# A hand-written scheduler counts TensorE's latency, gets more exponential slots and a new order in the second layer

## The chip, the cores and the metric

The kernel runs on one core of a Trainium2 chip, in one launch. The metric is the device time of a whole execution in microseconds. An engine is one of TensorE (PE; its weight loads are shown apart as PEld), VectorE (DVE), ScalarE (ACT), GpSimd (POOL) and SyncE (SP, which here only issues DMAs).

## The reference

Two layers, with the same weights in both. Each adds an attention block and then a token-mixing MLP to x, which is 2048 tokens by 512 features in bf16:

```python
x = x + _A_ref(_layernorm(x), A_wqkv, A_wo)            # attention
x = x + _B_ref(_layernorm(x), B_w1, B_b1, B_w2, B_b2)  # MLP over the tokens
x = x + _A_ref(_layernorm(x), A_wqkv, A_wo)
x = x + _B_ref(_layernorm(x), B_w1, B_b1, B_w2, B_b2)
```

The attention has 32 heads of width 16 and a sliding window: a query sees itself and the 255 tokens before it. The MLP normalises once more, multiplies along the token axis with w1 (2048 to 1792), adds b1, applies the tanh form of gelu, multiplies with w2 (1792 to 2048), adds b2, and the result is added to x.

## The kernel before

**Tiling.** x lies in 16 tiles of 128 tokens (`x_sb`), its normalised form in `xh_sb`, the transposed normalised form in `xhT` (two buffers of 512 tokens). Attention goes in quarters Q of 512 queries. In a quarter there are four groups t of eight heads and for each nine steps m, so 36 steps a quarter, 144 a layer, 288 in all. A step is three things in turn:

- `emit_scores` (line 581): TensorE computes scores in 64x64 cells of its array, into two of four PSUM banks; two steps alternate between the halves.
- `emit_exp` (line 592): one exponential on ScalarE over both banks, into one of NSLOT slots of `p_sb` (line 268; step n takes slot n modulo NSLOT), and then multiplications with the edge mask (line 609), on GpSimd or VectorE.
- `emit_pv` (line 630): TensorE multiplies the slot with V, adding up over the nine steps in banks 4 and 5. After the ninth, VectorE copies both banks out (line 319), and small DMAs bring the denominators together (`den_c`).

**Jobs beside the steps.** `job_k`, `job_q` (matmuls at line 454) and `job_v` (line 500) make projections, which VectorE or ScalarE masks and writes out (lines 464, 469); `job_normalise` and `job_outproj` (548) finish the quarter before; `job_transpose` fills `xhT`, at the very start through TensorE and afterwards by a DMA transpose that SP issues (line 435). They all share PSUM banks 6 and 7 in turn. In the MLP, `u_product` (752) makes the first product, some of it ahead of time in the last attention quarter, and `job_y` (789) the second: 14 matmuls for one tile of 128 output tokens, in two operations of 10 and 4. Four y products of the first layer are done in the dense stage, four at the seam of the layers, and eight inside the second layer's attention (tiles 8 to 11 and 12 to 15).

**What sets the order.** Every operation goes into `Plan` with a cost in ns for each engine that could do it, its reads and writes, and a priority. `Plan.arrange` then walks through all of them before the program is built: it keeps a clock for each engine, takes the engine that can go on first, and there the operation of lowest priority among those that are ready within 60 ns. TensorE has three modes (full, columns for V, cells for scores, PV and normalising), and an operation in another mode than the last counts as 1.0 later in priority and 100 ns longer. The result is a fixed order for each engine; on the chip semaphores hold the dependences, and an operation of TensorE that depends on an earlier one of TensorE waits for no semaphore. The line of the walk that the change touches is 151: `lat`, the time from an operation's end until a dependent may start, is 80 ns, and 200 for TensorE's operations, but before the change 0 from TensorE to TensorE.

**Priorities.** A step is 5/9 of a unit, a quarter 20 units, and the second layer begins at unit BASE = 400. Scores come EARLY = 1.0 unit ahead of a step's position, PV 1.6 behind it. `span_jobs` spreads a quarter's jobs evenly over 19 units in a written order ("k1" is the K projection of group 1, "K0" that of the next quarter's group 0, "v" the V projections of the next quarter, "o" the output projections of the quarter before), and `beside` says at which job the transposes are issued. The warm-up (line 394) is 13 blocks of ten small matmuls in bank 4, at -7.2, while the first inputs come in. `constants` has GpSimd write the ones beside V (`put_ones`), build `spread` (memset and 16 selects, lines 831 and 838) and load the two bias vectors (line 844).

Of the kernel before, what the change touches and what calls it, by code (L numbers as in the profile page):

```python
# [10 lines left out]
P = 128  # L11
EARLY = 1.0
PV_LAG = 1.6
FIRSTV = -0.7
WARM = 13
NPART = 4
PARTQ = (0, 1)
# [1 line left out]
MASKED = 1215  # L19
XPOS = 0.7  # L20
XSTEP = 1.2
NORM0 = 6.5
XLAT = 1500
SPAN0 = 0.3
SPAN = 19.0

# [13 lines left out]
class Plan:  # L40
# [53 lines left out]
    def arrange(self):  # L94
# [12 lines left out]
        todo = len(self.ops)  # L107
        while todo:
            best = None
            for e in self.ENGS:  # L110
                if not pool[e]:
                    continue
                t = max(free[e], min(o.ready for o in pool[e]))
                if best is not None and t >= best[0]:
                    continue
                pick = None
                for o in pool[e]:
                    if o.ready > t + 60:
                        continue
                    if any(max(free[x], o.ready) + w[0] + self.SPARE.get(x, 0) <  # L120
                           max(t, o.ready) + o.on[e][0] + self.SPARE.get(e, 0) for x, w in o.on.items() if x != e):
                        continue
                    key = (o.prio + (self.STAY if e == "tensor" and o.mode != mode else 0), o.num)
                    if pick is None or key < least:
                        pick, least = o, key
                if pick is not None:
                    best = (max(t, pick.ready), e, pick)
            if best is None:
                cand = min(((max(free[e], o.ready) + o.on[e][0] + self.SPARE.get(e, 0), o.num, e, o) for e in self.ENGS for o in pool[e]),
                           key=lambda v: v[:2])  # L130
                e, pick = cand[2], cand[3]
                best = (max(free[e], pick.ready), e, pick)
            t, e, o = best
            o.eng, o.start = e, t
            free[e] = t + o.on[e][0]
            if e == "tensor":
                if o.mode != mode:
                    free[e] += self.SWITCH
                mode = o.mode
            if o.dma:  # L140
                bus = max(bus, free[e]) + o.dma / 200
                o.end = bus + 1600
            else:
                o.end = free[e]
            line[e].append(o)
            for x in o.on:
                pool[x].remove(o)
            todo -= 1
            for s in o.succ:
                s.left -= 1  # L150
                s.ready = max(s.ready, o.end + (0 if e == "tensor" and e in s.on else o.lat))
                if not s.left:
                    for x in s.on:
                        pool[x].append(s)
# [80 lines left out]
def bass_interleave_layers__sliding_block__mixer_token_mlp__prompt_kernel(  # L235
# [16 lines left out]
    NQ = S // 512  # L252
    NFT = F // P
    EPS = 1e-5
    SMSCALE = 1.0 / math.sqrt(DH)
    NSLOT = 5

    es = ExitStack()
    with es:
# [171 lines left out]
        def job_transpose(Q, i, prio):  # L431

            t, buf = 4 * Q + i, Q % 2
            if prio > 0:
                plan.op({SP: (600, lambda e: e.dma_start_transpose(xhT[:, buf, :, i * P:(i + 1) * P], xh_sb[:, t, :]))},
                        reads=[R("xh", t)], writes=[R("xhT", buf, i)], prio=prio, dma=1 << 17, lat=XLAT)
                return
            b = misc_bank()
            pv = ps[:, b, :].bitcast(dt.bfloat16)
# [19 lines left out]
        def masked(b, prio, dst, src, mask, key, writes):  # L459
# [7 lines left out]
            def each(e):  # L467
                for h in range(2):
                    last = e.activation(dst[:, :, h], src, ACTF.Copy, scale=mask[:, h:h + 1])
                return last  # L470
            plan.op({ACT: (1380, each)} if key == "even" and prio < 0 else {DVE: (MASKED, both), ACT: (1380, each)}, reads=[R(key)], shares=[BK(b)], writes=writes, prio=prio)

        def job_k(Q, t, prio):

# [34 lines left out]
        def first_jobs(p0, dp):  # L509

            jobs = [lambda p, i=i: job_transpose(0, i, p) for i in range(4)] + [lambda p: job_k(0, 0, p), lambda p: job_q(0, 0, p)]
            return ([(p0 + dp * n, job) for n, job in enumerate(jobs)] +
                    [(p0 + 9 + FIRSTV + 0.3 * i, lambda p, i=i: job_v(0, i, p)) for i in range(4)])

        def span_jobs(Q, p0):


            order = ["k1", "q1", "v0", "v1", "k2", "q2", "v2", "o0", "k3", "q3", "o1", "v3", "K0", "Q0", "o2", "o3"]
            beside = {"q1": (0, 1), "q2": (2,), "k3": (3,)} if Q + 1 < NQ else {}
            if Q == 0:  # L520
                order = [j for j in order if j[0] != "o"]
            if Q == NQ - 1:
# [161 lines left out]
        def attention(L, base):  # L684
            todo, n = [], 0
            for Q in range(NQ):
                for t in range(4):
                    for m in range(NB):
# [4 lines left out]
                        todo.append((p0, step))  # L693
                        todo.append((p0 + PV_LAG, lambda p, a=(Q, t, m, n % NSLOT): emit_pv(*a, p)))
                        n += 1
                todo += span_jobs(Q, base + 20 * Q)
            end = base + 20 * NQ
            todo.append((end + 3, lambda p: job_inverse(NQ - 1, p)))
            for t in range(2):
# [120 lines left out]
                ln_stats(t, p)  # L820
            ln_apply(g, False, p)
        for g in range(NQ):
            todo.append((-20 if g == 0 else 18 * g - 19, lambda p, g=g: first_norm(g, p)))

        def constants(p):
            for n in range(2, 5):
                for i in range(2):
                    put_ones(n, i, p + 5 * n, [R("xh", 3)], (POOL,))


            setup(lambda e: e.memset(spread[:], 0.0), 530, reads=[R("xh", 3)], writes=[R("spread")], prio=p)
# [19 lines left out]
        for L in range(2):  # L851
# [23 lines left out]
                        todo.append((base + 126, lambda p, n=n, i=i: put_ones(n, i, p, engines=(POOL,), writes=[R("v", n, i, h) for h in range(2)])))  # L875
            for st in range(NT):
                p, b = base + 131 + st, st % 6
                if L == 0 and 4 <= st < 8:
                    p = BASE - 9 + 2.2 * (st - 4)
                elif L == 0 and st >= 8:  # L880
                    p = BASE + (8 + 3 * (st - 8) if st < 12 else 26 + 3 * (st - 12))
                    b = None
                todo.append((p, lambda p, st=st, b=b, L=L: job_y(st, misc_bank() if b is None else b, L, p)))
        todo.sort(key=lambda v: v[0])
        for p, job in todo:
# [32 lines left out]
```

## Time and profile before

| | |
|---|---|
| median of 3 runs | 533.8 us (533.21 to 535.61) |
| the profiled execution | 534.36 us, of which the span of instructions is 532.6 |
| granted TensorE clock, mean | 0.997 |
| first layer, attention (first to last exponential) | 17.7 to 177.8 us |
| then dense MLP and the seam of the layers | to 252.8 us |
| second layer, attention | 252.8 to 434.3 us |
| then dense MLP to the end | 532.6 us |

The mean exponential of full width (128 x 1024) takes 1.03 us on ScalarE. By quarter, from the first exponential of one to the first of the next, the time is 39.3, 41.6, 38.8 and 40.4 us in the first layer and 46.7, 54.4, 40.0 and 40.4 us in the second; the exponentials of a quarter are busy for 29.3 us in a first quarter, where they are shorter, and 36.8 to 37.1 us in the others. Busy times of TensorE overlap, since its matmuls are pipelined, so they say more as a comparison of stages than as a share.

### The profile page before, as it was taken

The page shows a single profiled execution, that of the slowest core. Times are in us where ns is not written, and L with a number is a line of the kernel's source. Part 1 is how long each engine was busy: PE and PEld are TensorE (multiplying, and loading weights), DVE is VectorE, ACT ScalarE, POOL GpSimd, SP SyncE. Part 2 cuts the span into 40 slices and gives each one's busy share as a digit, 9 for nine tenths or more (in the row PEclk, how much of TensorE's full clock was granted, in tenths as well). Part 3 has the DMA queues.
Part 4 walks back from the last instruction along what each step waited for, and adds up shares of the span by engine and source line. Part 5 has one row for each costly group of instructions (what it writes and reads, how often), then busy time and mean ns, then how long its engine had stood idle before and what let it go on. Part 6 is the DMA issues. An engine that isn't in the chain of part 4 may idle for free.

```text
span 532.6 us, 21297 instructions
## 1 busy us (share of the span) xinstructions
PE 484.0 (91%) x9540; PEld 273.7 (51%) x9618; DVE 318.7 (60%) x539; ACT 296.1 (56%) x335; POOL 234.4 (44%) x468
## 2 busy tenths in 40 slices
PE   7779889989889899999889888988998989999997
PEld 7455555655555444445545555555645544444443
DVE  5778869868767361157756767596876655221222
ACT  5757887988888304300746766479888860230000
POOL 5976864756665301101735644276565540200000
PEclk9999999999999999999999999999999999999999
DMA  6192515210135430533203410032221635053631
GB/s 198 45 121 66 103 44 97 72 45 25 45 96 158 124 108 0 138 103 78 43 3 94 105 31 25 3 53 73 83 65 57 192 113 149 1 140 97 180 113 44
DMA packets 84443, 44.38 MB, mean 83 GB/s; under 512 B 20864, under 2 KB 83328, under 8 KB 84352
## 3 DMA queue, kind: packets, MB, share of 16 engines
q1 hardware_dynamic: 80480, 43.00, 30.7%
q0 software_dynamic: 3872, 0.02, 1.9%
q8 instruction: 75, 1.23, 1.0%
q14 instruction: 16, 0.13, 0.1%
HBM read 32.51 MB, written 2.10 MB: 65 GB/s over the span
## 4 chain that ended last, share of the span: by engine, by line
PE 72%; DVE 12%; issue 7%; POOL 5%; ACT 3%; SPq 1%; DMA 0%; POOLq 0%; ACTq 0%; DVEq 0%
PE ps L789 18%; PE ps L752 18%; PE ps L581 9%; PE ps L454 8%; PE ps L630 8%; PE ps L548 5%; PE ps L500 4%; ACT p_sb L592 3%; DVE q_sb L464 2%; POOL p_sb L609 2%; DVE k_sb L464 1%; DVE xh_sb L417 1%; DVE oU L319 1%; POOL rstd L410 1%; PE ps L674 1%
## 5 line engine op out<-in xcount | busy, mean ns | idle before, releaser
L592 ACT ACTIVATE p_sb<-ps 128x1024 bf16<-128x1024 f32 (+8 forms) x288 | 261.3, 972 | 104.1 <-PE ps L581 96.3
L609 POOL TENSOR_TENSOR p_sb<-p_sb,edge 128x128 bf16<-128x128 bf16 (+2 forms) x361 | 171.8, 480 | 137.5 <-ACT p_sb L592 126.2
L581 PE MATMUL ps<-q_sb,k_sb 64*64 64x288 bf16 (+8 forms) x2816 | 106.9, 251 | 10.7 <-ACT p_sb L592 5.4
L630 PE MATMUL ps<-p_sb,v_all 64*64 64x288 bf16 (+8 forms) x2816 | 94.9, 248 | 11.1 <-POOL p_sb L609 6.0
L581 PEld LDWEIGHTS ps<-q_sb,k_sb 64*64 64x64 bf16 x2816 | 54.1, 106 | 60.5 <-ACT p_sb L592 29.7
L630 PEld LDWEIGHTS ps<-p_sb,v_all 64*64 64x64 bf16 x2816 | 58.4, 107 | 27.5 <-POOL p_sb L609 15.6
L793 DVE SCALAR_TENSOR_TENSOR x_sb<-ps,b2col,x_sb 128x512 bf16<-128x512 f32 x32 | 24.0, 750 | 76.0 <-PE ps L789 75.9
L454 PE MATMUL ps<-xhT,wqkv 128*128 128x512 bf16 x216 | 58.2, 384 | 9.8 <-issue 7.4
L789 PE MATMUL ps<-uT,w1buf 128*128 128x512 bf16 x274 | 61.8, 379 | 1.3 <-DVE rc L658 0.8
L464 DVE TENSOR_TENSOR k_sb<-ps,half 128x1024 bf16<-128x1024 f32 x32 | 39.0, 1218 | 16.1 <-PE ps L454 16.0
L752 PE MATMUL ps<-xh_sb,w1buf 128*128 128x512 bf16 x182 | 43.3, 379 | 2.0 <-issue 0.6
L400 DVE BATCH_NORM_STATS2 stats<-x_sb 128x6 f32<-128x512 bf16 x64 | 43.5, 688 | 1.1
L789 PEld LDWEIGHTS ps<-uT,w1buf 128*128 128x128 bf16 x280 | 26.8, 98 | 33.4 <-issue 1.8
L464 DVE TENSOR_TENSOR v_all<-ps,even 128x1024 bf16<-128x1024 f32 x29 | 35.1, 1217 | 11.5 <-PE ps L500 10.9
L464 DVE TENSOR_TENSOR q_sb<-ps,even 128x1024 bf16<-128x1024 f32 x31 | 37.7, 1217 | 4.5 <-PE ps L454 4.3
L410 POOL TENSOR_TENSOR rstd<-vare,mhalf 128x4 f32<-128x4 f32 x16 | 16.2, 1014 | 50.5 <-DVE nmean L412 50.4
L500 PE MATMUL ps<-wqkv,xhT 128*32 128x128 bf16 x2048 | 34.7, 220 | 3.7 <-issue 2.6
L789 PE MATMUL ps<-uT,oU 128*128 128x512 bf16 x165 | 36.8, 379 | 0.2
L454 PEld LDWEIGHTS ps<-xhT,wqkv 128*128 128x128 bf16 x256 | 20.5, 98 | 30.3 <-issue 7.8
L500 PEld LDWEIGHTS ps<-wqkv,xhT 128*32 128x32 bf16 x2048 | 29.1, 97 | 9.9 <-issue 7.2
L779 ACT ACTIVATE uT<-ps,b1col 128x512 bf16<-128x512 f32 x20 | 13.3, 689 | 36.8 <-PE ps L752 36.8
L548 PE MATMUL ps<-wo_sb,oT 128*128 128x512 bf16 x117 | 29.9, 380 | 2.9 <-DVE oT L681 1.7
(67 smaller groups left out, 396.2 us busy)
## 6 DMA issues: line engine op xcount, KB each, us to landing
w1buf<-in_B_w_dram SPq DMA_DIRECT2D x10, 896.0 KB
oU<-in_B_w_dram SPq DMA_DIRECT2D x6, 896.0 KB
w1buf<-in_B_w_dram SPq DMA_DIRECT2D x10, 512.0 KB
oU<-o SPq DMA_DIRECT2D x16, 256.0 KB
k_sb<-in_B_w_dram SPq DMA_DIRECT2D x16, 256.0 KB
xhT<-in_B_w_dram SPq DMA_DIRECT2D x8, 256.0 KB
q_sb<-in_B_w_dram SPq DMA_DIRECT2D x8, 256.0 KB
out_dram<-x_sb SPq DMA_DIRECT2D x16, 128.0 KB
```

The costliest lines, as they stand in the source:

```text
L400: dve(lambda e: e.bn_stats(stats[:, t, :], x_sb[:, t, :]), 690, prio, reads=[R("x", t)], writes=[R("stats", t)])
L454: last = e.matmul(ps[:, b, :], lhsT=wqkv[:, c, c0:c0 + P], rhs=xhT[:, buf, c, :], start=(c == 0), stop=(c == 3))
L464: return e.tensor_tensor(dst, src.unsqueeze(2).to_broadcast([P, n, 2, w]), mask[:].unsqueeze(1).unsqueeze(3).to_broadcast([P, n, 2, w]), o ...
L500: last = e.matmul(acc[32 * a:32 * a + 32, k], lhsT=xhT[:, buf, c, t0:t0 + 32], rhs=wv[:, c, :, a, :], start=(k == 0 and c == 0), stop=(k = ...
L548: last = e.matmul(ps[:, b, :], lhsT=oT[:, buf, t, i * P:(i + 1) * P], rhs=wo_sb[:, t, :], start=(t == 0), stop=(t == 3))
L581: last = e.matmul(ps[64 * c:64 * c + 64, 2 * half + r, 32 * i0:32 * i1], lhsT=k_sb[rows, ring, t, kb % 16, :], rhs=q_sb[rows, t, c, 32 * i ...
L592: latest[0] = plan.op({ACT: (170 + int(2 * (512 - c0) * 0.84), lambda e: e.activation(p_sb[:, slot, :, c0:512], ps[:, 2 * half:2 * half + ...
L609: return e.tensor_tensor(v, v, g, op=ALU.mult)
L630: last = e.matmul(ps[64 * r:64 * r + 64, B_O + (c ^ r), 32 * i0:32 * i1], lhsT=v_all[rows, col:col + 64], rhs=p_sb[rows, slot, r, 32 * i0: ...
L752: r = e.matmul(ps[:, b, :], lhsT=blk[:, n, (ft % 2) * P:(ft % 2 + 1) * P], rhs=xh_sb[:, 4 * g + n, :], start=(first and g == quarters[0] a ...
L789: r = e.matmul(ps[:, b, :], lhsT=blk[:, fc, (st % 2) * P:(st % 2 + 1) * P], rhs=uT[:, fc, :], start=(fc == 0), stop=(fc == NFT - 1))
L793: dve(lambda e: e.scalar_tensor_tensor(x_sb[:, st, :], ps[:, b, :], b2col[:, st:st + 1], x_sb[:, st, :], op0=ALU.add, op1=ALU.add), 750, prio,
```

## The change

Seven things are changed:

- In the walk, a dependence from TensorE to TensorE now counts the 200 ns too.
- NSLOT is 7 instead of 5.
- A DMA transpose takes 1230 ns of SP in the walk and has the usual latency of 80, instead of 600 and 1500.
- `spread` and the bias loads have a priority 10 units later.
- In the second layer `span_jobs` has an order of its own, in which all K and Q projections come first and V jobs alternate with output projections; the four transposes are issued together at "q3". The last quarter keeps its order.
- y products of the first layer that lie in the second layer's attention have new positions: tiles 8 to 11 at 10, 13, 16 and 19 units (before: 8, 11, 14, 17) and tiles 12 to 15 at 31, 34, 37 and 40 (before: 26, 29, 32, 35). Tiles 4 to 7 stay.
- FIRSTV, VACT and NORM1 become parameters, with values that give what was written out before.

```diff
@@ -11,7 +11,13 @@
 P = 128
 EARLY = 1.0
 PV_LAG = 1.6
-FIRSTV = -0.7
+FIRSTV = (-0.7, -0.4, -0.1, 0.2)
+VACT = 0
+NORM1 = -1
+SPREADP = 10
+ORDER1 = "k1 q1 k2 q2 k3 q3 v0 o0 v1 o1 o2 v2 o3 v3 K0 Q0"
+BES1 = {"q3": (0, 1, 2, 3)}
+YP = ((-9, 2.2), (10, 3), (31, 3))
 WARM = 13
 NPART = 4
 PARTQ = (0, 1)
@@ -20,7 +26,6 @@
 XPOS = 0.7
 XSTEP = 1.2
 NORM0 = 6.5
-XLAT = 1500
 SPAN0 = 0.3
 SPAN = 19.0
 
@@ -148,7 +153,7 @@
             todo -= 1
             for s in o.succ:
                 s.left -= 1
-                s.ready = max(s.ready, o.end + (0 if e == "tensor" and e in s.on else o.lat))
+                s.ready = max(s.ready, o.end + o.lat)
                 if not s.left:
                     for x in s.on:
                         pool[x].append(s)
@@ -253,7 +258,7 @@
     NFT = F // P
     EPS = 1e-5
     SMSCALE = 1.0 / math.sqrt(DH)
-    NSLOT = 5
+    NSLOT = 7
 
     es = ExitStack()
     with es:
@@ -432,8 +437,8 @@
 
             t, buf = 4 * Q + i, Q % 2
             if prio > 0:
-                plan.op({SP: (600, lambda e: e.dma_start_transpose(xhT[:, buf, :, i * P:(i + 1) * P], xh_sb[:, t, :]))},
-                        reads=[R("xh", t)], writes=[R("xhT", buf, i)], prio=prio, dma=1 << 17, lat=XLAT)
+                plan.op({SP: (1230, lambda e: e.dma_start_transpose(xhT[:, buf, :, i * P:(i + 1) * P], xh_sb[:, t, :]))},
+                        reads=[R("xh", t)], writes=[R("xhT", buf, i)], prio=prio, dma=1 << 17)
                 return
             b = misc_bank()
             pv = ps[:, b, :].bitcast(dt.bfloat16)
@@ -468,7 +473,7 @@
                 for h in range(2):
                     last = e.activation(dst[:, :, h], src, ACTF.Copy, scale=mask[:, h:h + 1])
                 return last
-            plan.op({ACT: (1380, each)} if key == "even" and prio < 0 else {DVE: (MASKED, both), ACT: (1380, each)}, reads=[R(key)], shares=[BK(b)], writes=writes, prio=prio)
+            plan.op({ACT: (1380, each)} if key == "even" and prio < VACT else {DVE: (MASKED, both), ACT: (1380, each)}, reads=[R(key)], shares=[BK(b)], writes=writes, prio=prio)
 
         def job_k(Q, t, prio):
 
@@ -510,13 +515,16 @@
 
             jobs = [lambda p, i=i: job_transpose(0, i, p) for i in range(4)] + [lambda p: job_k(0, 0, p), lambda p: job_q(0, 0, p)]
             return ([(p0 + dp * n, job) for n, job in enumerate(jobs)] +
-                    [(p0 + 9 + FIRSTV + 0.3 * i, lambda p, i=i: job_v(0, i, p)) for i in range(4)])
-
-        def span_jobs(Q, p0):
+                    [(p0 + 9 + FIRSTV[i], lambda p, i=i: job_v(0, i, p)) for i in range(4)])
+
+        def span_jobs(Q, p0, L):
 
 
             order = ["k1", "q1", "v0", "v1", "k2", "q2", "v2", "o0", "k3", "q3", "o1", "v3", "K0", "Q0", "o2", "o3"]
             beside = {"q1": (0, 1), "q2": (2,), "k3": (3,)} if Q + 1 < NQ else {}
+            if L == 1 and ORDER1:
+                order = ORDER1.split()
+                beside = {} if Q + 1 == NQ else BES1
             if Q == 0:
                 order = [j for j in order if j[0] != "o"]
             if Q == NQ - 1:
@@ -693,7 +701,7 @@
                         todo.append((p0, step))
                         todo.append((p0 + PV_LAG, lambda p, a=(Q, t, m, n % NSLOT): emit_pv(*a, p)))
                         n += 1
-                todo += span_jobs(Q, base + 20 * Q)
+                todo += span_jobs(Q, base + 20 * Q, L)
             end = base + 20 * NQ
             todo.append((end + 3, lambda p: job_inverse(NQ - 1, p)))
             for t in range(2):
@@ -820,12 +828,13 @@
                 ln_stats(t, p)
             ln_apply(g, False, p)
         for g in range(NQ):
-            todo.append((-20 if g == 0 else 18 * g - 19, lambda p, g=g: first_norm(g, p)))
+            todo.append((-20 if g == 0 else 18 * g - 18 + NORM1, lambda p, g=g: first_norm(g, p)))
 
         def constants(p):
             for n in range(2, 5):
                 for i in range(2):
                     put_ones(n, i, p + 5 * n, [R("xh", 3)], (POOL,))
+            p += SPREADP
 
 
             setup(lambda e: e.memset(spread[:], 0.0), 530, reads=[R("xh", 3)], writes=[R("spread")], prio=p)
@@ -875,11 +884,10 @@
                         todo.append((base + 126, lambda p, n=n, i=i: put_ones(n, i, p, engines=(POOL,), writes=[R("v", n, i, h) for h in range(2)])))
             for st in range(NT):
                 p, b = base + 131 + st, st % 6
-                if L == 0 and 4 <= st < 8:
-                    p = BASE - 9 + 2.2 * (st - 4)
-                elif L == 0 and st >= 8:
-                    p = BASE + (8 + 3 * (st - 8) if st < 12 else 26 + 3 * (st - 12))
-                    b = None
+                if L == 0 and st >= 4:
+                    p0, dp = YP[st // 4 - 1]
+                    p = BASE + p0 + dp * (st % 4)
+                    b = None if p >= BASE else b
                 todo.append((p, lambda p, st=st, b=b, L=L: job_y(st, misc_bank() if b is None else b, L, p)))
         todo.sort(key=lambda v: v[0])
         for p, job in todo:
```

## The prediction

> **What bounds the kernel now.** I read the page first, then the busy times in ten stretches cut where the exponentials of one quarter of an attention layer begin (36 steps each), then ScalarE's and TensorE's timelines inside the bad stretches.
>
> ```profile
> span 532.6 us, 21297 instructions
> PE 484.0 (91%) x9540; PEld 273.7 (51%) x9618; DVE 318.7 (60%) x539; ACT 296.1 (56%) x335; POOL 234.4 (44%) x468
> ```
>
> The 91% is a mean over stages with different limits, so it decides nothing. The stretches do (columns: length, then busy PE, PEld, DVE, ACT, POOL, clock):
>
> ```profile
> 17.70:57.00 39.30, 32.25 (x914) 19.34 (x912) 30.64 (x55) 29.25 (x42) 29.16 (x74) 0.96 0.64 82
> 98.60:137.40 38.80, 35.08 (x1084) 22.71 (x1084) 29.48 (x45) 34.66 (x37) 24.62 (x45) 1.00 0.15 47
> 177.80:252.80 75.00, 74.53 (x544) 34.86 (x549) 31.51 (x57) 11.87 (x16) 8.61 (x12) 1.00 0.33 90
> 252.80:299.50 46.70, 41.45 (x972) 24.24 (x974) 31.80 (x48) 27.18 (x36) 25.36 (x68) 1.00 0.24 59
> 299.50:353.90 54.40, 48.88 (x1197) 29.17 (x1207) 37.77 (x60) 34.73 (x38) 27.00 (x50) 1.00 0.13 29
> 434.30:532.60 98.30, 94.65 (x502) 42.91 (x509) 26.67 (x44) 11.04 (x15) 3.75 (x6) 1.00 0.36 103
> ```
>
> The dense stages (third and last row) are TensorE without a gap, 49 matmuls in 10.74 us on the chain, or 219 ns each: an order can win nothing there. A plain quarter (second row) has 34.7 us of ScalarE in 38.8: the exponentials, 36 of 1.03 us, are its floor. The two quarters of the second layer that carry four y products each take 46.7 and 54.4 us although ScalarE is busy for 27.2 and 34.7 and TensorE idles 5 us in each: neither engine is the bound, they take turns. The timeline shows how:
>
> ```profile
> 270.71 3.20 PE L789 MATMUL ps<-uT,w1buf 128*128 128x512 bf16 x14
> 273.96 0.81 PE L454 MATMUL ps<-xhT,wqkv 128*128 128x512 bf16 x3
> 275.07 1.14 ACT L592 ACTIVATE p_sb<-ps 128x576 bf16<-128x576 f32 x2 [3.41 <-PE ps L581]
> 284.40 2.33 PE L789 MATMUL ps<-uT,w1buf 128*128 128x512 bf16 x10
> 286.67 0.43 PE L581 MATMUL ps<-q_sb,k_sb 64*64 64x288 bf16 x8
> 287.03 1.14 ACT L592 ACTIVATE p_sb<-ps 128x576 bf16<-128x576 f32 x2 [1.68 <-PE ps L581]
> 287.71 0.81 PE L789 MATMUL ps<-uT,w1buf 128*128 128x512 bf16 x3 [0.16 <-issue]
> 288.91 2.69 ACT L592 ACTIVATE p_sb<-ps 128x1024 bf16<-128x1024 f32 x3 [0.74 <-PE ps L581]
> ```
>
> A whole y product (14 matmuls in one piece) holds TensorE for 3.2 us and ScalarE starves for 3.41. One of the eight happens to be cut into its 10 and its 4, with scores between: 1.68 + 0.74 = 2.42. The other six whole ones cost 1.87, 2.55, 2.86, 4.41, 3.53 and 4.18: the mean of the seven is 3.26.
>
> The first quarter has a loss of its own:
>
> ```profile
> 39.24 1.04 PE L454 MATMUL ps<-xhT,wqkv 128*128 128x512 bf16 x2 [2.58 <-issue]
> 40.90 1.89 ACT L592 ACTIVATE p_sb<-ps 128x1024 bf16<-128x1024 f32 x2 [4.02 <-PE ps L581]
> 40.00:44.00 4.00, 4.00 (x81) 2.13 (x84) 3.17 (x4) 2.25 (x3) 1.47 (x4) 0.68 0.02 4
> ```
>
> TensorE stands 2.58 us inside a product, waiting for nothing shown, and then runs at a granted 0.68. Just before, from 32.5 to 36.2 us, the two bias loads moved 3872 packets of 4 bytes; TensorE's instruction-fetch packets of 16 KB, normally 4 to 7 us apart here, start at 29.7 and only then at 36.8.
>
> **The change, part by part.** The sum is made against the profiled execution, 534.36 us (span 532.6 and 1.8 around it), 0.6 above the median of 533.8. Edits that leave every value as it was (FIRSTV, VACT, NORM1) cost nothing.
>
> *TensorE's 200 ns in the walk.* The walk now holds a TensorE operation back for 200 ns after the one it depends on. At the start, the 13 warm-up blocks form such a chain. By the code's costs (three of 1070, ten of 540, now 200 between) the first transpose is ready when ten are placed, not thirteen; one more falls among the transposes, one before the first K and one before the first Q. In the trace the blocks run to 10.34 and the transposes begin at 10.40, though their first input was normalised by about 9.0. A block is about 0.56 us, so K can start up to 1.5 us sooner and Q, with one block ahead of it, 0.9. Q gates the first scores: **-0.9** (0 to -1.5).
>
> In the y products the gap lies between the 10 and the 4. If scores take it, a whole y goes from 3.26 to 2.42 us of starving: 7 x 0.84 = 5.9. But the walk adds 1.0 to the priority of anything that changes TensorE's mode, so another K or Q product, if one is ready, takes the gap instead; four of the eight y products are followed directly by a K, Q or output projection now. Half: **-3.0** (0 to -5.9). The four pairs of u products that run in one piece (one followed by 1.81 us of ScalarE idle, another by 1.39) give **-0.5**.
>
> The same gap lies between any two PV operations. The order of weight loads in the trace has 106 of 288 PVs directly behind another. What fills the gap is scores if ScalarE has freed a bank, else a projection, ahead of the scores it used to follow. One product more before the scores costs 0.5 us where it shows (0.51 to 0.58 in four places). How often is not in the trace: between none and thirty, 0 to +15. I take three, **+1.5**, because the products are the same in number and two banks limit how far they run ahead.
>
> Each change of mode also costs. Four projection matmuls followed by another full product take 0.86 us, followed by scores 0.97: 0.11. Seven cuts are 14 changes at most, 1.5 us, mostly inside TensorE's 5 us of idle per quarter: **+0.5**. The Trainium skill (TensorEngine Tiling (Array Packing), Key Properties) says that changing the tiling mode drains the engine, which speaks against every cut; the trace agrees, at 0.11 us. Without that price the sum is 0.5 lower.
>
> *Seven slots.* ScalarE waits for a PV, that is for a slot, six times: 1.02 in the first quarter, then 0.92, 0.79, 0.82, 0.75 and 1.52, together 4.8. With 7 slots the next exponential needs a PV two steps older. But PVs wait there for VectorE's copies out of their two banks, which stay: half, **-2.4** (0 to -4.8).
>
> *Spread and bias loads 10 units later.* GpSimd's selects no longer go before the edge masks: the first PV waits 0.86 us for one, and the exponential behind it 1.02. VectorE is busy 4.00 of 4.00 us from 24 to 28, so it is late next: **-0.5** (0 to -1.0). The bias loads move with them, past masks on GpSimd's queue (their two issues hold it 1.3 and 1.2 us). The stall of 2.6 us comes back if a fetch falls due in their 3.7 us; at 4 to 7 us between fetches that is more likely than not, but with a shorter delay on average: **-1.5** (-4.0 to +2.6). The Trainium skill (Runtime: NRT & Kernel Launch, Instruction fetch mechanics) has fetches in blocks of 16 KB, mostly hidden; the trace has the 16 KB packets, and a stall beside a late one.
>
> *Second layer's order, y later.* The amount of work is the same. V pairs that run in one piece (1.9 us at 264.2 and at 305.5, the latter followed by 1.38 of ScalarE idle) come apart. The fourth y of each group slides towards the next quarter, where TensorE idles 4 of 40 us. Against it, three or four y products gather in a half quarter with four V jobs. **-1.0** (-3 to +3). V must precede the next quarter's first PV at unit 21.6; V3 at 15.7 leaves six units, some 14 us.
>
> *Transposes.* SP's row is 1.24 us for each and their packets end 2.0 us after issue begins; the walk's new 1230 + 655 + 1600 + 80 is still longer, the old 4355 more so. No V will wait: **0**. The four now go in one burst past the den_c loads on SP, 5 us, hidden by the 6 units above.
>
> Sum: -0.9 - 3.0 - 0.5 + 1.5 + 0.5 - 2.4 - 0.5 - 1.5 - 1.0 = -7.8, so 526.6 for a profiled execution and **526.0** for the median.
>
> **Rivals.**
> *The gaps go to projections (slower).* If thirty of the 106 PV gaps take a product ahead of scores, 30 x 0.52 = +15.6 in place of the +1.5 gives 526.0 + 14.1 = 540. It decides from about 18 such places (7.8 + 1.5 over 0.52). For it: the walk's delay is not the chip's (two PVs back to back take 0.46 us, two single ones 0.22 each). Against: only two banks feed products.
> *Nothing that can be told.* Projections take the y gaps too, the slots' waits reappear as VectorE's copies, the fetch stall recurs: left are the start and half of the rest, -2, 532. Under 0.5% (2.7 us) no measurement of this kernel tells a change; the changed constants would then have done what they say for nothing.
> *The stall is no fetch.* Then moving the bias loads returns 0: 526.0 + 1.5 = 527.5. This is also what the Trainium skill's word "hidden" would make of it. For it: shorter unexplained stops elsewhere (1.60 us at 266.4). Against: the packets' times.
>
> **How the numbers follow.** Forecast 0.45, no fetch 0.12, nothing to tell 0.17, projections 0.26. So faster 0.57, same 0.17, slower 0.26. The range: down to the forecast with the y cut, slots and bias terms nearly whole (-3, -2.4, -2.5 more: 518), up to 541, the slower rival and 1; about 0.2 is outside.
>
> **What would show it.** Fewer than 13 warm-up blocks before the first transpose, and the first exponential near 16.8 instead of 17.74. y products in 10 and 4 with scores between, and the second layer's first two quarters below 46.7 and 54.4 us. No ScalarE wait ended by a PV. TensorE without a 2.6 us stop near 36 to 45 us. Dense stages unchanged. Wrong if plain quarters grow beyond 41.6 us with projections between PVs, or those two stay at 101 us together.

## The result, and the profile after

The changed kernel takes 525.97 us (median of 4, 525.07 to 528.41) where the kernel before took 534.59 (median of 4): a ratio of 0.9853 [0.9832, 0.9875], so about 1.5% faster, or 7.8 us of 533.8. (The two medians alone would give 0.984; the text goes by the ratio.) The forecast was 526.0. The profiled execution took 525.07 us, span 523.3, 9.3 us less than the 532.6 before. The mean granted clock was 0.997 before and 0.999 after, so the clock explains next to nothing; only in the first quarter do the rows differ, 0.96 before and 1.00 after.

The page after, span and engines:

```profile
span 523.3 us, 21380 instructions
PE 492.1 (94%) x9618; PEld 275.1 (53%) x9618; DVE 317.6 (61%) x533; ACT 297.7 (57%) x337; POOL 236.3 (45%) x473
```

The same work as before in a shorter span: only the shares rise. Where the 9.3 us went is seen in the stretches cut as before (columns: length, then busy PE, PEld, DVE, ACT, POOL, clock). These are the first and third quarter of the first layer, the dense stage with the seam, the second layer's first three quarters, and the dense end:

```profile
18.30:54.00 35.70, 32.30 (x1001) 20.37 (x990) 32.30 (x50) 28.10 (x40) 29.86 (x78) 1.00 0.66 102
95.40:135.10 39.70, 36.76 (x1037) 22.41 (x1032) 30.76 (x46) 34.58 (x36) 24.79 (x45) 1.00 0.15 45
173.30:249.60 76.30, 75.36 (x551) 34.86 (x549) 31.39 (x60) 11.87 (x16) 9.18 (x14) 1.00 0.33 89
249.60:293.10 43.50, 41.57 (x976) 23.86 (x972) 29.75 (x42) 27.39 (x36) 25.41 (x69) 1.00 0.20 46
293.10:342.90 49.80, 46.43 (x1177) 27.55 (x1172) 37.10 (x60) 34.81 (x36) 27.35 (x49) 1.00 0.16 42
342.90:386.00 43.10, 40.77 (x1166) 24.81 (x1158) 34.75 (x52) 35.81 (x39) 27.42 (x50) 1.00 0.33 66
424.90:523.30 98.40, 95.35 (x512) 42.91 (x510) 26.67 (x44) 11.02 (x15) 3.75 (x6) 1.00 0.36 103
```

The first quarter fell from 39.2 to 35.7, the second layer's first two from 46.7 and 54.4 to 43.5 and 49.8, and its third rose from 40.0 to 43.1. The dense stages did not gain: the end is 98.3 and 98.4, the seam 75.1 and 76.3. To two decimals, from exponential to exponential, in us:

| | first exp. | first layer, quarters 1 to 4 | seam | second layer, quarters 1 to 4 | end |
|---|---|---|---|---|---|
| before | 17.74 | 39.23, 41.62, 38.78, 40.38 | 75.10 | 46.69, 54.33, 40.03, 40.37 | 98.34 |
| after | 18.28 | 35.69, 41.41, 39.76, 38.12 | 76.34 | 43.55, 49.79, 43.02, 38.90 | 98.48 |
| change | +0.54 | -3.54, -0.21, +0.98, -2.26 | +1.24 | -3.14, -4.54, +2.99, -1.47 | +0.14 |

The changes add up to -9.3: -5.0 in the first layer's attention, -6.2 in the second's, +1.9 elsewhere. They are those of one execution each: the first quarter takes 37.1 to 39.2 us in four kernels in which no edit touches the first layer (the kernel before, `b_order_y`, `b_ypos`, `b_order1`).

ScalarE's waits have the slots' part (columns: engine, its operation, who it waited for; us in total, times, longest). Before, then after:

```profile
ACT p_sb L592 <- PE ps L581: 96.3, 83, 26.2
ACT p_sb L592 <- PE ps L630: 5.8, 6, 1.5
```

```profile
ACT p_sb L600 <- PE ps L589: 90.6, 86, 27.2
ACT p_sb L600 <- PE ps L638: 0.6, 1, 0.6
```

Each first row is the wait for scores (26.2 and 27.2 us of it is one wait through the dense stage), each second the wait for a PV, that is for a slot: 5.8 us have become 0.6, and without the long wait the one for scores fell from 70.1 to 63.4. So both kinds of starving shrank. That this fits the forecast's sum does not show that its terms were right; the experiments took them one by one. Every ratio below is against the kernel before, run on the same chip; the first four experiments shared one chip, the next four another, and the rest ran on two more, so a difference between ratios of different groups is an estimate. Medians count every run, while the ratios leave out four that were slow: 533.34 us of `a_nolat_y`, 534.78 of `b_order1`, and 580.93 and 588.31 of `b_bias90` (granted clock 0.85 and 0.82).

### The profile page after: what moved, and what is told of

The parts are those of the page before. It is cut to its first block, busy times and chain, and to the rows that moved or that the text cites. A ratio compares the mean times of both kernels' runs of the same rounds, so it can differ in the third digit from the quotient of the medians.

```text
span 523.3 us, 21380 instructions
## 1 busy us (share of the span) xinstructions
PE 492.1 (94%) x9618; PEld 275.1 (53%) x9618; DVE 317.6 (61%) x533; ACT 297.7 (57%) x337; POOL 236.3 (45%) x473
## 4 chain that ended last, share of the span: by engine, by line
PE 79%; DVE 8%; POOL 3%; issue 3%; ACT 3%; DMA 2%; SPq 1%; POOLq 0%; DVEq 0%; ACTq 0%
PE ps L760 19%; PE ps L797 19%; PE ps L589 10%; PE ps L459 9%; PE ps L638 9%; PE ps L556 6%; PE ps L505 5%; ACT p_sb L600 2%; PE ps L399 2%; POOL p_sb L617 2%; DMA oU<-o 1%; PE ps L682 1%; DVE oT L689 1%; DVE o L324 1%; DVE q_sb L469 1%
## 5 line engine op out<-in xcount | busy, mean ns | idle before, releaser
L617 POOL TENSOR_TENSOR p_sb<-p_sb,edge 128x256 bf16<-128x256 bf16 (+2 forms) x366 | 173.1, 478 | 127.5 <-ACT p_sb L600 116.2
L589 PE MATMUL ps<-q_sb,k_sb 64*64 64x288 bf16 (+8 forms) x2816 | 108.5, 250 | 7.2 <-ACT p_sb L600 6.0
L638 PE MATMUL ps<-p_sb,v_all 64*64 64x288 bf16 (+8 forms) x2816 | 104.9, 247 | 10.7 <-issue 3.4
L638 PEld LDWEIGHTS ps<-p_sb,v_all 64*64 64x64 bf16 x2816 | 60.1, 107 | 30.9 <-POOL p_sb L617 13.2
L459 PE MATMUL ps<-xhT,wqkv 128*128 128x512 bf16 x256 | 65.9, 381 | 1.9 <-DVE v_all L469 0.8
L797 PE MATMUL ps<-uT,w1buf 128*128 128x512 bf16 x280 | 63.7, 379 | 0.0
L760 PE MATMUL ps<-xh_sb,w1buf 128*128 128x512 bf16 x192 | 45.5, 380 | 0.1
L469 DVE TENSOR_TENSOR k_sb<-ps,half 128x1024 bf16<-128x1024 f32 x31 | 37.6, 1214 | 7.9 <-PE ps L459 7.7
L556 PE MATMUL ps<-wo_sb,oT 128*128 128x512 bf16 x128 | 32.2, 381 | 0.9 <-DVE oT L689 0.9
```

The costliest lines, as they stand in the source:

```text
L459: last = e.matmul(ps[:, b, :], lhsT=wqkv[:, c, c0:c0 + P], rhs=xhT[:, buf, c, :], start=(c == 0), stop=(c == 3))
L469: return e.tensor_tensor(dst, src.unsqueeze(2).to_broadcast([P, n, 2, w]), mask[:].unsqueeze(1).unsqueeze(3).to_broadcast([P, n, 2, w]), o ...
L556: last = e.matmul(ps[:, b, :], lhsT=oT[:, buf, t, i * P:(i + 1) * P], rhs=wo_sb[:, t, :], start=(t == 0), stop=(t == 3))
L589: last = e.matmul(ps[64 * c:64 * c + 64, 2 * half + r, 32 * i0:32 * i1], lhsT=k_sb[rows, ring, t, kb % 16, :], rhs=q_sb[rows, t, c, 32 * i ...
L617: return e.tensor_tensor(v, v, g, op=ALU.mult)
L638: last = e.matmul(ps[64 * r:64 * r + 64, B_O + (c ^ r), 32 * i0:32 * i1], lhsT=v_all[rows, col:col + 64], rhs=p_sb[rows, slot, r, 32 * i0: ...
```

## The experiments

**One part alone, on the kernel before.** Three kernels each add one part; the fourth adds the second layer's order and the later y products together.

`b_lat`, the walk's line alone:

```diff
-                s.ready = max(s.ready, o.end + (0 if e == "tensor" and e in s.on else o.lat))
+                s.ready = max(s.ready, o.end + o.lat)
```

> The kernel before with one line changed: the walk counts 200 ns from TensorE to TensorE. Theory 1 (cut y products feed ScalarE): most of the 8.6 us comes from here, 528 to 531, with the gain in the second layer's first two quarters (101 us before, 96 to 98 then), plain quarters unchanged within 1 us. Theory 2 (PVs no longer follow one another, so scores come sooner everywhere): also 528 to 531, but the gain spread over all eight quarters, about 0.5 us in each. Rival (the line pays only with seven slots, since PVs now lag): 534 or slower, with more ScalarE waits ended by a PV than six.

Measured: 536.16 us, ratio 1.0034 [0.9978, 1.0091]. Alone, the latency gains nothing that can be told. Its trace says what it costs; ScalarE's waits in it:

```profile
ACT p_sb L592 <- PE ps L581: 87.9, 72, 27.2
ACT p_sb L592 <- PE ps L630: 13.1, 15, 2.0
```

The wait for scores, again without its longest, fell from 70.1 to 60.7 us, and the wait for PVs rose from 5.8 to 13.1, by 7.3; another 3.1 us are put down to GpSimd's masks. With other work between them the PVs come later behind their exponentials, and five slots run out: from the end of an exponential to the first weight load of its PV the median is 1.8 us before and 2.8 here (2.8 to 3.0 in the four kernels with the latency on PVs, 1.8 to 1.9 in the other ten). What the gaps give, the slots take.

`b_ylat`, the 200 ns only between the 10 and the 4 matmuls of a y product:

```diff
-                s.ready = max(s.ready, o.end + (0 if e == "tensor" and e in s.on else o.lat))
+                s.ready = max(s.ready, o.end + (0 if e == "tensor" and e in s.on and not (o.mode == "full" and o.lat == 201) else o.lat))
...
-                pe(f, 217 * (hi - lo), prio, ...)
+                pe(f, 217 * (hi - lo), prio, ...).lat = 201
```

> The kernel before, with the 200 ns counted only from the first ten matmuls of a y product to its last four. Theory 1: 530 to 532 (prediction's term -3.0), the y products cut by scores, 101 us of the two quarters down to about 98. Theory 2 (the PV gaps matter): no change, 534 to 535.

Measured: 538.67 us, ratio 1.0074 [1.0025, 1.0124], slower. In the second layer's first quarter scores take all four cuts; in the second (54.3 us before, 56.9 now) a projection takes three of the four. Here are the second of the three on TensorE's timeline (start, length, instruction), then the second and third on ScalarE's (with the idle time before it in brackets):

```profile
329.37 2.32 PE L789 MATMUL ps<-uT,w1buf 128*128 128x512 bf16 x10
331.53 1.03 PE L454 MATMUL ps<-xhT,wqkv 128*128 128x512 bf16 x4
332.39 1.03 PE L789 MATMUL ps<-uT,w1buf 128*128 128x512 bf16 x4
```

```profile
333.82 1.94 ACT L592 ACTIVATE p_sb<-ps 128x1024 bf16<-128x1024 f32 x2 [4.49 <-PE ps L581]
339.06 1.94 ACT L592 ACTIVATE p_sb<-ps 128x1024 bf16<-128x1024 f32 x2 [3.30 <-PE ps L581]
```

Ten matmuls, a K or Q projection, four matmuls, and ScalarE has starved for 4.49 us. That is what an uncut y product with a projection behind it cost before (3.41 to 4.41): the cut gains nothing there. The first of the three loses: it starves ScalarE for 4.22 us, where the uncut product was followed by scores and cost 2.86. The start (0.8 us later) and the seam (1.1 more) hold most of the rest of this trace's 4.4 us.

`b_slots`:

```diff
-    NSLOT = 5
+    NSLOT = 7
```

> The kernel before with seven slots. Prediction's term: 532 (-2.4), the six ScalarE waits ended by a PV (5.8 us) gone. Rival (those waits come back as waits for scores behind the same PV): 534 to 535, the waits ended by PV gone but waits ended by scores longer by as much.

Measured: 530.39 us, ratio 0.9936 [0.9884, 0.9989]. No ScalarE wait ends with a PV any more. The slots alone gain about 3.4 us, with the interval from 0.6 to 6.2.

`b_order_y`, the second layer's order with its burst of transposes, and the y products' places:

```diff
+            if L == 1:
+                order = "k1 q1 k2 q2 k3 q3 v0 o0 v1 o1 o2 v2 o3 v3 K0 Q0".split()
+                beside = {} if Q + 1 == NQ else {"q3": (0, 1, 2, 3)}
...
-                    p = BASE + (8 + 3 * (st - 8) if st < 12 else 26 + 3 * (st - 12))
+                    p = BASE + (10 + 3 * (st - 8) if st < 12 else 31 + 3 * (st - 12))
```

> The kernel before with the second layer's new order, the burst of transposes and the later y products, nothing else. Prediction's term: 533.5 (-1.0). Rival A (PV and y blocks in one piece make the later y products collide with V jobs): 536 to 538. Rival B (the order is what pays): 530 or faster, in the second layer's first three quarters.

Measured: 527.69 us, ratio 0.988 [0.983, 0.993]: nearly the whole gain of the change, from the part that the forecast put at 1.0 us. The first three quarters of its second layer:

```profile
252.00:295.70 43.70, 41.31 (x988) 24.01 (x976) 28.41 (x38) 27.25 (x36) 25.60 (x71) 1.00 0.17 43
295.70:345.40 49.70, 47.76 (x1185) 27.92 (x1188) 37.81 (x62) 33.98 (x36) 26.86 (x50) 1.00 0.21 44
345.40:390.10 44.70, 40.66 (x1152) 24.73 (x1141) 34.74 (x53) 34.74 (x37) 25.32 (x46) 0.96 0.26 64
```

43.7 and 49.7 are what the changed kernel has (43.5 and 49.8), without the latency and without the slots. So those two quarters fell by the order and the y places, not by the latency's cuts. (Three of the eight y products are cut in this trace all the same, where one was before.)

**One part taken back, on the changed kernel, and two more on the kernel before.** `a_nolat` is the changed kernel with the old line of the walk:

```diff
-                s.ready = max(s.ready, o.end + o.lat)
+                s.ready = max(s.ready, o.end + (0 if e == "tensor" and e in s.on else o.lat))
```

> The changed kernel with the walk's 0 ns from TensorE to TensorE put back. Theory S (slots and the second layer's order are the whole gain, as their runs alone, -4.1 and -6.8, suggest): 523 to 527, the same as the changed kernel or a little faster. Theory I (the latency pays once there are seven slots): 529 or slower, PVs in one piece again (about 110 pairs).

Measured: 528.67 us, ratio 0.9917 [0.989, 0.9945], against 0.9853 [0.9832, 0.9875] with the latency. There the latency is worth 0.64%, 3.4 us; the two intervals do not overlap. The last quarter of the first layer shows a part of it. Without the latency (`a_nolat`), TensorE's timeline and ScalarE's:

```profile
156.09 1.04 PE L556 MATMUL ps<-wo_sb,oT 128*128 128x512 bf16 x4 [0.47 <-DVE oT L689]
156.96 1.89 PE L760 MATMUL ps<-xh_sb,w1buf 128*128 128x512 bf16 x8
158.78 0.65 PE L589 MATMUL ps<-q_sb,k_sb 64*64 64x32 bf16 x24
```

```profile
159.26 3.00 ACT L600 ACTIVATE p_sb<-ps 128x1024 bf16<-128x1024 f32 x3 [2.34 <-PE ps L589]
```

With it (the changed kernel), the same:

```profile
153.85 1.04 PE L760 MATMUL ps<-xh_sb,w1buf 128*128 128x512 bf16 x4
154.82 0.65 PE L589 MATMUL ps<-q_sb,k_sb 64*64 64x32 bf16 x24
155.31 0.39 PE L638 MATMUL ps<-p_sb,v_all 64*64 64x224 bf16 x8
155.63 1.04 PE L760 MATMUL ps<-xh_sb,w1buf 128*128 128x512 bf16 x4
156.59 0.41 PE L589 MATMUL ps<-q_sb,k_sb 64*64 64x96 bf16 x12
```

```profile
155.31 2.85 ACT L600 ACTIVATE p_sb<-ps 128x1024 bf16<-128x1024 f32 x3 [0.53 <-PE ps L589]
158.60 2.85 ACT L600 ACTIVATE p_sb<-ps 128x1024 bf16<-128x1024 f32 x3 [0.44 <-PE ps L589]
```

A projection and two u products in one piece hold TensorE for 2.7 us and ScalarE starves for 2.34; cut by scores, it starves for 0.53 and, ahead of the K that follows, 0.44. This quarter takes 38.1 to 38.7 us in all four kernels with the full latency or with all but its y part, and 40.0 to 40.4 in the others, those with it between y parts alone included. Not all of that difference is gained: in the four kernels one u product more, four matmuls, is done in the quarter before, which takes 39.4 to 39.9 us there and 37.8 to 39.1 in the others. The two quarters together take 79.1 us in `a_nolat` and 77.9 in the changed kernel, so 1.2 of the 3.4 us lie here. Another 2.3 lie in the first layer's second quarter (43.7 and 41.4), and no run shows why. Each change from such a product to scores costs 0.1 us here too: four matmuls take 0.97 from 153.85 to 154.82, and 0.87 ahead of another product from 156.09 to 156.96.

`a_slots5` is the changed kernel with five slots:

```diff
-    NSLOT = 7
+    NSLOT = 5
```

> The changed kernel with five slots. The latency alone made 15 ScalarE waits ended by a PV, 13.1 us, where there had been 7 and 5.9. If slots are what repairs that: 532 to 536 and about as many waits ended by a PV. If slots only add their own 4 us: 530.

Measured: 530.14 us, ratio 0.9942 [0.992, 0.9963]. Five slots cost 0.89%, 4.7 us, and ScalarE's waits in it say why:

```profile
ACT p_sb L600 <- PE ps L638: 8.0, 12, 1.4
```

Here 12 waits for a PV stand against one of 0.6 us: the latency needs the slots.

`b_slots_order` has the edits of `b_slots` and `b_order_y` together:

```diff
-    NSLOT = 5
+    NSLOT = 7
...
+            if L == 1:
+                order = "k1 q1 k2 q2 k3 q3 v0 o0 v1 o1 o2 v2 o3 v3 K0 Q0".split()
...
+                    p = BASE + (10 + 3 * (st - 8) if st < 12 else 31 + 3 * (st - 12))
```

> The kernel before with seven slots and the second layer's order and y positions; no latency, spread and bias loads early, the old transpose cost. If the two add up: 534.5 - 4.1 - 6.8 = 523.6, faster than the changed kernel, and the other parts cost 2 us together. If they remove the same idle time: 526 to 528.

Measured: 528.56 us, ratio 0.9927 [0.9889, 0.9964]. If the two single ratios multiplied it would be 0.982. They do not: to seven slots the order adds nothing that can be told (0.9936 to 0.9927), and to the order the seven slots add nothing either.

`b_ypos` has only the y products' places of `b_order_y`:

```diff
-                    p = BASE + (8 + 3 * (st - 8) if st < 12 else 26 + 3 * (st - 12))
+                    p = BASE + (10 + 3 * (st - 8) if st < 12 else 31 + 3 * (st - 12))
```

> The kernel before with only the eight y products 2 and 5 units later. If the place of the y products is what makes the order's gain: 528 to 530, the second layer's second quarter near 50 us and its third near 44. If it is the order of V and output projections: 534 to 536.

Measured: 534.59 us, ratio 1.0023 [0.9993, 1.0054], no change. The second and third quarter of the second layer:

```profile
298.60:351.30 52.70, 48.43 (x1191) 28.34 (x1189) 38.26 (x63) 34.34 (x37) 26.42 (x48) 1.00 0.20 41
351.30:395.40 44.10, 39.87 (x1124) 23.31 (x1120) 34.35 (x54) 34.55 (x37) 26.53 (x50) 1.00 0.28 65
```

1.6 us less in one (54.3 before), 4.1 more in the other (40.0): The later y products take time out of one quarter and leave more in the next, though no y matmul lies there: one projection more does, and ScalarE idles 9.6 us in it where it idled 5.3. The changed kernel's +2.99 is of the same kind (four y matmuls and two projections more than before); how the places cost the third quarter so much is not shown.

**Finer parts.** `b_order1` has only the order and the burst, without the y places:

```diff
+            if L == 1:
+                order = "k1 q1 k2 q2 k3 q3 v0 o0 v1 o1 o2 v2 o3 v3 K0 Q0".split()
+                beside = {} if Q + 1 == NQ else {"q3": (0, 1, 2, 3)}
```

> The kernel before with only the second layer's new order of jobs and the burst of four transposes; the y products stay at their old places. With the y places it gave a ratio of 0.988, the y places alone 1.002. If the order is the gain: 0.986 to 0.991, the second layer's first two quarters near 95 us together (before 101.0, order and places 93.4). If it needs the y products out of the V jobs' way: 0.997 to 1.005.

Measured: 531.31 us, ratio 0.995 [0.9917, 0.9982]. The second quarter of its second layer (54.4 before) is

```profile
300.00:351.70 51.70, 49.77 (x1205) 28.82 (x1198) 39.39 (x64) 34.96 (x37) 30.68 (x55) 1.00 0.14 32
```

and its third stays at 40.2. So the order does gain without the y places, about 2.7 us with an interval from 1.0 to 4.4. Which element of it gains (K and Q first, V and output projections in turn, or the burst) was not tried.

`a_nolat_y` is the changed kernel with the 200 ns everywhere but between the parts of a y product:

```diff
-                s.ready = max(s.ready, o.end + o.lat)
+                s.ready = max(s.ready, o.end + (0 if o.lat == 201 and e in s.on else o.lat))
...
-                pe(f, 217 * (hi - lo), prio, ...)
+                pe(f, 217 * (hi - lo), prio, ...).lat = 201
```

> The changed kernel, but no 200 ns between the two parts of a y product; it stays between all other operations of TensorE. Prediction's step (cuts of y feed ScalarE, 3 to 6 us): slower, 528 to 532. Rival (a projection takes the cut, as in the kernel where only y had the 200 ns, 1.007): 523 to 525, faster than the changed kernel's 526.

Measured: 526.81 us, ratio 0.9868 [0.9834, 0.9902]: the changed kernel, within what can be told. Its second layer's first two quarters together take 93.7 us, the changed kernel's 93.3. But half of the eight y products are cut here as well, by the order of what else is ready. One that is, and one that is not:

```profile
325.62 2.33 PE L797 MATMUL ps<-uT,w1buf 128*128 128x512 bf16 x10
328.89 1.04 PE L797 MATMUL ps<-uT,w1buf 128*128 128x512 bf16 x4
335.07 3.19 PE L797 MATMUL ps<-uT,w1buf 128*128 128x512 bf16 x14
```

Of the four that the 200 ns cut in the changed kernel, projections take three. So the 200 ns between the parts are worth nothing that can be told; what a cut as such is worth, this run does not say.

`b_bias90` was meant to take the bias loads away from the fetch at 36.8 us, with a priority 90 units later:

```diff
+            p += 90
```

> The kernel before with only the two bias loads at priority 90, in the dense stage; spread stays early. In seven kernels with bias packets from 31 to 38 us TensorE stops 1.1 to 2.6 us at 38 to 40 us, each time until 2.2 to 2.6 us after a late fetch packet. If the bias packets hold up the fetch: no stop there, a first quarter of 36 to 37.5 us (before 39.2), 531 to 532. If the fetch is late for another reason: the stop stays and the time too.

Measured: 531.38 us, ratio 0.9953 [0.9928, 0.9978]. It gives no answer: their packets stayed at 33.5 to 38.6 us, because the walk gives an idle GpSimd whatever is ready, however late its priority. The stop near 39 us fell to 1.03; why, and why the kernel is 0.5% faster, is not known.

`b_bias_late` makes them a job of their own that depends on the latest exponential, at priority 85:

```diff
+        def biases(p):
...
-                        writes=[R(key)], prio=p, dma=1 << 13)
+                        writes=[R(key)], prio=p, dma=1 << 13, after=latest)
+        todo.append((85, biases))
```

> The kernel before with only the two bias loads held back until the first layer's last exponential, so that their 3872 packets move in the dense stage (a later priority alone had left them at 33.5 to 38.6 us). If the bias packets hold up TensorE's instruction fetch: no stop of TensorE from 36 to 42 us, a first quarter of 36 to 37 us (37.1 to 39.2 in kernels of the same order), ratio 0.993 to 0.997; at most a stop in the dense stage, where 256 instructions last over 25 us. If a fetch is late there for another reason: the stop stays and the ratio is 0.998 to 1.002.

Measured: 531.72 us, ratio 0.9983 [0.9962, 1.0005]. The packets now move at 177.8 to 180.5 us, and TensorE still stops at the old place:

```profile
37.05 0.49 PE L630 MATMUL ps<-p_sb,v_all 64*64 64x288 bf16 x16
39.08 0.59 PE L454 MATMUL ps<-xhT,wqkv 128*128 128x512 bf16 x2 [1.54 <-DVE agg L401]
```

The releaser named, VectorE's aggregate, ran from 38.05 to 38.22 us; the instruction fetch before the stop starts at 36.8 us, 2.3 us ahead of the restart, just where it started before the stop of 2.58. The bias packets are gone from there and fetch and stop are not, so the bias loads are not what delays it.

## Why the prediction was right in its sum and wrong in its terms

The sum was -7.8 and the measured ratio of 0.9853 is -7.8 of 533.8. That they agree is luck: several terms are far off, some too large and some too small, and the errors cancel. The terms, one at a time (differences of ratios times 533.8):

| term | predicted | shown |
|---|---|---|
| start | -0.9 | first exponential 0.54 later; with an unchanged start it lies anywhere from 17.63 to 18.85 |
| y cuts | -3.0 | the 200 ns in y alone +3.9; in the changed kernel -0.8, not told from 0 |
| u pairs | -0.5 | -1.2 in the first layer's last two quarters together |
| the whole latency (start, y, u, PV gaps, modes) | -2.4 | alone +1.8, not told from 0; in the changed kernel -3.4 |
| seven slots | -2.4 | alone -3.4; in the changed kernel -4.7 |
| order and y places | -1.0 | alone -6.4; with seven slots -0.5, not told from 0; never taken out of the changed kernel |
| `spread`, bias loads, transposes | -2.0 | -0.5 (`b_slots_order` to `a_nolat`), not told from 0 |

**The y cuts: the step that failed.** The forecast took the second layer's first two quarters for the sum of whole y products at 3.26 us of starving, and priced a cut at 0.84 less. The changed kernel's eight cuts came: five take scores and PVs, one a projection and then scores, two a K, Q or output projection alone. One cut as announced, TensorE then ScalarE:

```profile
322.81 2.33 PE L797 MATMUL ps<-uT,w1buf 128*128 128x512 bf16 x10
325.07 0.41 PE L589 MATMUL ps<-q_sb,k_sb 64*64 64x192 bf16 x12
327.67 1.04 PE L797 MATMUL ps<-uT,w1buf 128*128 128x512 bf16 x4
328.55 1.03 PE L556 MATMUL ps<-wo_sb,oT 128*128 128x512 bf16 x4
```

```profile
325.56 3.04 ACT L600 ACTIVATE p_sb<-ps 128x1024 bf16<-128x1024 f32 x3 [1.37 <-PE ps L589]
329.97 1.94 ACT L600 ACTIVATE p_sb<-ps 128x1024 bf16<-128x1024 f32 x2 [1.37 <-PE ps L589]
```

1.37 + 1.37 is 2.74 us where an uncut product cost 3.26. It is the dearest of the five that scores took (1.94 to 2.74 for the two waits together, mean 2.29), because its four last matmuls still lie in front of a projection; the three that a projection took cost 2.74, 3.12 and 3.70, which lies among the 1.87 to 4.41 of the uncut ones before. So the price of a cut that scores take was about right. What failed is what it was counted against. In `a_nolat`, with the new order and no latency, three of the eight are cut anyway, and the five whole ones cost 2.45 to 3.24, mean 2.79, since only two have a projection behind them. Its two quarters take 93.7 us and the changed kernel's 93.3: beside the new order little was left for the cuts to gain. With the old order the gap let projections in (`b_ylat`). The step treated what fills the gap as a chance of one half; it should have asked, product by product, what else is ready there. The announced sign (those two quarters below 46.7 and 54.4) came true for another reason, the order.

**The order: the term that was mis-sized.** -1.0 was taken since the amount of work is the same. Alone the order gains 2.7, with the y places 6.4 (3.7 to 9.1). The y places do not gain alone: the fourth y product of a group was to slide into the next quarter's idle TensorE; at most four of its matmuls did, and that quarter grew by 3.0 us all the same (4.1 in `b_ypos`, 4.7 in `b_order_y`). That is also a sign of being wrong that the forecast named: a plain quarter beyond 41.6 us, 43.0 here. The latency's gaps are not its cause, since `b_order_y` and `b_slots_order` have 44.7 and 44.1 without them.

**Slots and gaps were priced apart, and they are one term.** The forecast booked PV gaps at +1.5 and slots at -2.4 as if independent. The gaps delay the PVs (1.8 to 2.8 us behind their exponentials), the PVs free the slots: with the latency there are 15 and 12 waits for a PV on five slots (`b_lat`, `a_slots5`), and one on seven. Each alone is worth at most 3.4 us, and taking back either from the changed kernel costs 3.4 or 4.7.

**What held.** The slots' own mechanism, as said: the waits went from 5.8 us to 0.6. The u pairs, with the size too small. The dense stages did not move, apart from 1.2 us more at the seam. There the last four matmuls of a y product had lain between the first K and Q projections and the V jobs. Now all y matmuls come ahead of K and Q, and V waits for VectorE's copy of K. Before, then after:

```profile
247.80 1.89 PE L454 MATMUL ps<-xhT,wqkv 128*128 128x512 bf16 x8
249.53 1.03 PE L789 MATMUL ps<-uT,oU 128*128 128x512 bf16 x4
```

```profile
244.34 1.89 PE L459 MATMUL ps<-xhT,wqkv 128*128 128x512 bf16 x8
247.00 2.21 PE L505 MATMUL ps<-wqkv,xhT 128*32 128x128 bf16 x128 [0.76 <-DVE k_sb L469]
```

The seam is 76.0 to 76.3 us in the five kernels with any of the latency, 75.9 in `a_nolat`, and 75.1 in the other eight. The warm-ups went as worked out, ten before the first transposes, then one, one and one:

```profile
9.65 0.61 PE L448 MATMUL ps<-ident,xh_sb 128*128 128x128 bf16 x8
12.20 1.02 PE L459 MATMUL ps<-xhT,wqkv 128*128 128x512 bf16 x4 [0.22 <-ACT xhT L326]
```

The transposes came 0.75 us sooner (10.40 before), K 0.96 sooner (13.16), and yet the first exponential came later, at 18.28. The gain was lost ahead of ScalarE's first exponential: it masked two V jobs ahead of it where it had masked one:

```profile
15.84 2.56 ACT L474 ACTIVATE v_all<-ps,even 128x512 bf16<-128x512 f32 x4
18.28 1.02 ACT L600 ACTIVATE p_sb<-ps 128x1024 bf16<-128x1024 f32 x1
```

**The rivals.** "The gaps go to projections" was right on the mechanism for the y products (1.0074 alone) and wrong on its place: PVs directly behind a PV fell from 106 to 45, and seven slots kept that from costing. "The stall is no fetch" has the packets' times against it in every trace. Its price, 0 for moving the bias loads, is not told from the forecast's -1.5: holding them back alone measured -0.9 us (+0.3 to -2.0).

**Readings that do not hold.** The six waits for a slot add up to 5.8 us; 4.8 is without the first, which the spread term has. The floor of a plain quarter is not 36 times 1.03 us: these durations overlap, and the exponentials of a full quarter keep ScalarE busy for 34.3 to 34.7 us. The bias packets stand at 33.0 to 36.9 us, not 32.5 to 36.2. And 7.1 us from one fetch to the next is not late by itself: the two that start at 51.9 and 59.1 us are 7.2 apart, with no stop above 0.6 us behind them.

## What to carry to other kernels

A planner's gap is only as good as the work that is ready to fill it: list it place by place, since a gap between two parts of a long product helps where scores are ready and gains nothing, or loses, where another product is. Buffers and delays around the same resource are one term: price the pair, and expect parts that gain nothing alone and do not add up together. A right sum of seven terms confirms none of them; only taking one away does.

## What the runs showed of the hardware

TensorE's stops without a shown reason go with its instruction packets, so its instructions seem to come late. In the 14 traces of this study every such stop above 0.6 us inside the attention ends 2.2 to 3.0 us (once 3.5) after a 16 KB instruction packet starts, and from the start of the packet before to the start of that one TensorE began 237 to 501 matmuls and weight loads. The count alone does not tell them apart: the packets of the attention with no such stop behind them have 16 to 431, with a median of 255, and those with one a median of 312. The stops add up to 4.2 us in the changed kernel's trace and 8.2 before. The largest one after:

```profile
67.41 0.61 PE L638 MATMUL ps<-p_sb,v_all 64*64 64x64 bf16 x22
70.29 0.24 PE L638 MATMUL ps<-p_sb,v_all 64*64 64x128 bf16 x2 [2.27 <-issue]
```

Its packet starts at 67.8 us, 6.7 us and 470 of these instructions after the one at 61.1. So moving the `spread` and bias operations did not remove the loss: the stop near 39 us is gone in the changed kernel and its three variants and there in all the others (1.0 to 2.6 us), but those four have another of 1.95 to 2.81 between 58 and 76 (`b_lat` has both). What makes a fetch late stays open. The Trainium skill (Runtime: NRT & Kernel Launch, Instruction fetch mechanics) gives 256 instructions to a block of 16 KiB and says that the cost of crossing a block's end is mostly hidden. What is not hidden is 3.6 to 10.6 us in 13 of the 14 traces, 0.7 to 2% of the span, and 1.4 in `b_bias_late`, or 3.0 with the stop of 1.54. One block being run through before the next has come would fit these counts, but no run shows it.
